# First linear-attention layer computed through G (input times phi of keys), with GpSimd making parts of the keys

## The chip, the cores and the metric

The program runs on one core of a Trainium2 chip. The metric is the device time of one execution in microseconds. Three executions of the kernel before took 1737.16, 1738.05 and 1738.56 us; the median, 1738.05 us, is what the changed kernel is compared with.

## The reference

Four layers in the order A, B, A, B are applied to x of shape 2048 x 640 (32 heads of 20 columns), each as `x = x + layer(layernorm(x))`. Layer A is linear attention with one set of weights for both of its uses:

```python
phi = lambda t: jnp.where(t > 0, t + 1, jnp.exp(t)) + 1e-6
pq, pk = phi(q), phi(k)                      # q, k, v = x @ wqkv, by head
kv = jnp.einsum("bhsd,bhse->bhde", pk, v)
z = jnp.einsum("bhsd->bhd", pk)
num = jnp.einsum("bhqd,bhde->bhqe", pq, kv)
den = jnp.einsum("bhqd,bhd->bhq", pq, z)[..., None] + 1e-6
return (num / den) @ wo
```

Layer B splits the sequence into four segments of 512 rows. Each segment has causal softmax attention by head and, mixed in by a gate, a read of a memory that the earlier segments have written. Nothing of layer B's arithmetic is touched here.

## The kernel before

**Pieces.** x lives in DRAM between layers. A segment is 512 rows, four tiles of 128 rows. Matmuls with f32 accuracy are made of f16 pairs: a value is split into a high and a low f16 part, and three products (high*high, high*low, low*high) are accumulated. `proj_n` (L388) makes one half tile of a projection in natural layout, 128 rows by 320 columns, with 5 x 3 = 15 matmuls of 320 columns; I call this a chain. `proj_t` (L374) makes 128 output columns by 512 rows, transposed, with 15 matmuls of 512 columns. `turn` (L312) transposes a tile with five f32 transposes and writes both f16 parts (ACT the high one, DVE the low one).

**The two ways to compute layer A.** The first layer A uses `a_first` (L695). For each segment it makes values (8 chains, evacuated by one ACT instruction each into v), phi of keys (8 chains, then exponential and relu on ACT, minimum and +1e-6 on GpSimd at L421, sum on DVE at L422) and phi of queries (5 `proj_t`, the same phi at 512 columns, stored to DRAM by GpSimd's queue at L721), and adds phi(keys)^T v, f32 matmuls of 147 or 168 columns (L730), into `acc`. Its second half, `a_second` (L802), reads the queries back, multiplies them with the memory (`a_read` L759 into `read_mem` L439: f32 matmuls at L450, then reciprocal and product on DVE), turns the result and projects it with wo (`o_half` L471).

The second layer A uses `g_first` (L522). Values are never made. For each segment it makes phi of keys (`keys`, 8 chains; ACT exponential and relu, DVE sum at L410, ACT the high f16 part times k_scl at L537, DVE the low part at L538, DVE adds to z at L543), phi of queries in natural layout (`queries`, 8 chains, DVE adds 1e-6 at L549, SP stores to DRAM), and adds x^T phi(keys) into G (`memory`, 10 chains of 12 matmuls at L564; the last operand needs all four tiles of keys). `xs` holds the f16 parts of the normalized x in natural layout, its low part made by GpSimd (L513). After the fourth segment `merge` (L588) scales G by 1/z, multiplies it with wv (L642) and then with wo (L674, L679) into one matrix `wm`. Its second half reads the queries, multiplies them by z and by the reciprocal of their head sums on GpSimd (`p_read` L766: L771, L777, with three small DVE instructions between), turns them and projects with `wm`.

**Order of the work.** PE's instructions run in program order; the order on the other engines is made by a scheduler at build time. The program weaves generators: `weave` (L98) alternates the chains of a main generator with pieces of an auxiliary one. In `opening` (L1149) the main one is the first layer's first half, segment by segment, and the auxiliary ones prepare the eight weight matrices (`w_prep` L228: DMA in, five maximum reductions on DVE at L239, a transpose and a broadcast through PE at L247 and L253, five ACT copies at L263 and five DVE differences at L264, DMA out) and normalize the next segment's x (`moments` L333: two DVE statistics at L338, a power on GpSimd at L343; `normed` L366 on ACT). Before the first chain stand the first tile's transposes and the whole preparation of the first weight. When `opening` has ended, `dense` (L1226) weaves the second half of layer A with layer B's projections (`b_project` L865) segment by segment. A second stream, layer B's attention, starts when B's first segment is projected; `run` (L1307) alternates the streams by accumulated cost. GpSimd masks each exponential tile of the attention (L1059), and PE's weighted sums (L1075) need the masked tile.

The first layer B weaves `b_out` of segment 0 (eight chains, 20 transposes) into the projection of segment 2; the second layer B stores that segment's result instead and does `b_out` at the end. Otherwise both layers B have one form.

## Time and profile before

| what | value |
|---|---|
| median of three runs | 1738.05 us |
| profiled execution, device time | 1736.07 us |
| its span, first to last instruction | 1734.4 us |
| PE busy | 1666.1 us, 96% of the span |
| DVE busy | 1180.9 us, 68% |
| ACT busy | 969.7 us, 56% |
| GpSimd (POOL) busy | 517.7 us, 30% |
| granted TensorE clock | 0.998 |

Times in the rows are microseconds from the start of the span. In the chain of waits and the timeline a row gives its start, its length, the engine, the line and the number of merged records; an f32 matmul that is not a transpose has two records. In groups of instructions the mean of one instruction is in ns, and it includes pipelining: consecutive matmuls follow each other faster than one of them lasts, so that the cost of a chain is read from the chain of waits, where rows follow each other without overlap.

### The profile page before, as it was taken

What the parts mean: (1) busy time and instruction counts of PE and PEld (TensorE: products, weight loads), DVE (VectorE), ACT (ScalarE), POOL (GpSimd) and SP (SyncE); (2) the same over time, 40 slices, a digit from 0 to 9 for tenths busy, and PEclk for the clock granted to TensorE, in tenths of its full rate; (3) what the DMA queues carried; (4) which work ended last, traced back from release to release, by engine and by line L of the source; (5) the groups of instructions that cost most, each with busy time, mean ns of one, the idle gap of its engine ahead of it and who ended that gap; (6) DMA issues with size and microseconds to landing.
All of it is one profiled execution on the core that took longest, in us unless ns stands there. A gap on an engine that the chain in (4) does not pass through costs nothing.

```text
span 1734.4 us, 36014 instructions
## 1 busy us (share of the span) xinstructions
PE 1666.1 (96%) x13032; PEld 1047.5 (60%) x13032; DVE 1180.9 (68%) x3849; ACT 969.7 (56%) x1818; POOL 517.7 (30%) x982
## 2 busy tenths in 40 slices
PE   6999999999999999999999999999999999999998
PEld 4676667664565576556556777666546545645555
DVE  8645534577787677759864456746777877878773
ACT  5545433357557645667675544333665576666673
POOL 1543350012123312334351301221422432233452
PEclk9999999999999999999999999999999999999999
DMA  7522452422322322352211303423232323223432
GB/s 262 184 109 95 150 195 97 139 76 82 113 71 73 113 96 68 120 179 95 78 48 51 103 32 122 175 98 116 75 102 85 112 81 108 93 82 111 131 115 92
DMA packets 118330, 187.58 MB, mean 108 GB/s; under 512 B 13949, under 2 KB 79613, under 8 KB 115849
## 3 DMA queue, kind: packets, MB, share of 16 engines
q1 hardware_dynamic: 105896, 142.68, 25.5%
q0 software_dynamic: 3040, 21.63, 3.4%
q10 hardware_dynamic: 9216, 20.98, 3.1%
q8 instruction: 103, 1.69, 0.4%
q14 instruction: 75, 0.61, 0.1%
HBM read 106.05 MB, written 78.64 MB: 106 GB/s over the span
## 4 chain that ended last, share of the span: by engine, by line
PE 78%; DVE 10%; ACT 6%; issue 2%; POOL 2%; DMA 1%; SPq 1%; ACTq 0%; POOLq 0%; DVEq 0%
PE ps L395 32%; PE ps L381 17%; PE ps L1075 7%; PE ps L1048 4%; ACT pe L1052 3%; PE ps L1007 3%; PE ps L319 3%; PE ps L564 3%; PE ps L450 3%; DVE ps L1013 2%; PE ps L1088 1%; PE ps L891 1%; PE ps L730 1%; DVE st L338 1%; DVE xn L479 1%
## 5 line engine op out<-in xcount | busy, mean ns | idle before, releaser
L1013 DVE CUSTOM_DVE_ANT_0 ps<-ps,maskw 128x512 f32<-128x512 f32 (+3 forms) x1024 | 472.5, 519 | 38.0 <-PE ps L1007 35.7
L1052 ACT ACTIVATE pe<-ps,lsc 128x512 f32<-128x512 f32 x640 | 394.8, 696 | 87.6 <-PE ps L1048 84.9
L1059 POOL TENSOR_SCALAR_AFFINE_SELECT pe<-pe 128x256 f32<-128x256 f32 (+1 forms) x640 | 229.7, 365 | 449.2 <-ACT pe L1052 444.0
L395 PEld LDWEIGHTS <-xT 128*128 128x128 f16 x2880 | 280.3, 98 | 114.6 <-issue 9.3
L395 PEld LDWEIGHTS <-oT 128*128 128x128 f16 x1920 | 185.7, 98 | 80.5 <-issue 7.0
L1075 PE MATMUL ps<-pe,v 128*32 128x512 f32 (+3 forms) x2048 | 162.2, 436 | 11.5 <-POOL pe L1059 5.1
L395 PE MATMUL ps<-w_Bo,oT 128*128 128x320 f16 x960 | 142.3, 302 | 2.8 <-ACT pe L1052 1.1
L1013 DVE DVE_READ_ACCUMULATOR2_ANT mg<- 128x1 f32 x1024 | 143.9, 141 | 0.0
L381 PE MATMUL ps<-xT,w_Bq 128*128 128x512 f16 x600 | 140.2, 380 | 1.9 <-ACT pe L1052 0.8
L395 PE MATMUL ps<-w_Bv,xT 128*128 128x320 f16 x960 | 139.7, 300 | 0.8 <-DVE otok L1095 0.6
L381 PE MATMUL ps<-xT,w_Bk 128*128 128x512 f16 x600 | 138.8, 380 | 1.2 <-ACT pe L1052 1.2
L395 PE MATMUL ps<-w_Ak,xT 128*128 128x320 f16 x960 | 136.1, 300 | 0.0
L1007 PE MATMUL ps<-ks,qs 60*128 60x512 f16 (+3 forms) x1024 | 123.1, 298 | 6.7 <-ACT pe L1052 2.9
L856 DVE SCALAR_TENSOR_TENSOR nat<-ps,nat 128x512 f16<-128x512 f32 x80 | 55.2, 690 | 89.2 <-ACT nat L855 89.1
L1048 PE MATMUL ps<-qs,ks 62*128 62x512 f16 (+3 forms) x1024 | 105.9, 301 | 3.0 <-DMA qs<-mt 1.5
L1075 PEld LDWEIGHTS ps<-pe,v 128*32 128x32 f32 x2048 | 65.3, 109 | 71.9 <-issue 45.8
L421 POOL TENSOR_SCALAR e<-e 128x320 f32<-128x320 f32 (+1 forms) x52 | 82.9, 1594 | 82.4 <-ACT e L417 78.2
L855 ACT ACTIVATE nat<-ps 128x512 f16<-128x512 f32 x80 | 48.2, 603 | 91.8 <-PE ps L381 69.2
L381 PEld LDWEIGHTS <-w_Bk 128*128 128x128 f16 x600 | 57.3, 98 | 65.5 <-issue 5.6
L381 PEld LDWEIGHTS <-w_Bq 128*128 128x128 f16 x600 | 56.7, 98 | 65.9 <-issue 7.8
L1007 PEld LDWEIGHTS <-qs 60*128 60x128 f16 x1024 | 50.0, 94 | 70.9 <-issue 44.7
L343 POOL TENSOR_TENSOR rs<-rs,mhalf 128x1 f32<-128x1 f32 x48 | 27.0, 563 | 218.8 <-DVE rs L342 218.7
(217 smaller groups left out, 2630.7 us busy)
## 6 DMA issues: line engine op xcount, KB each, us to landing
x<-xn ACTq DMA_DIRECT2D x48, 320.0 KB
qs<-qd SPq DMA_DIRECT2D x128, 120.0 KB
ks<-kd SPq DMA_DIRECT2D x128, 120.0 KB
xo<-x SPq DMA_DIRECT2D x48, 320.0 KB
pqi<-pqd SPq DMA_DIRECT2D x32, 320.0 KB
qd<-nat SPq DMA_DIRECT2D x40, 256.0 KB
kd<-nat SPq DMA_DIRECT2D x40, 256.0 KB
x<-in_A_x SPq DMA_DIRECT2D x16, 320.0 KB
```

The costliest lines, as they stand in the source:

```text
L319: nc.tensor.transpose(pt[:, (c - c0) * P:(c - c0 + 1) * P], src[:, c * P:(c + 1) * P], self.ident)
L381: nc.tensor.matmul(p, w[:, c, a, t * P:(t + 1) * P], xT[:, c, b, :], start=k == 0, stop=k == 3 * C - 1)
L395: nc.tensor.matmul(p, xT[:, c, a, i * P:(i + 1) * P], w[:, c, b, n * HN:(n + 1) * HN], start=k == 0, stop=k == 3 * C - 1)
L421: nc.gpsimd.tensor_scalar(e, e, 1.0, eps, op0=OP.min, op1=OP.add)
L450: nc.tensor.matmul(nd[:, lo - k * cut:hi - k * cut], pq[t], mem[:, OFF[t] + lo - a:OFF[t] + hi - a], start=first, stop=True, skip_group_ch ...
L856: nc.vector.scalar_tensor_tensor(nat[:, 1], p, QK_SHIFT, nat[:, 0], op0=OP.mult, op1=OP.subtract)
L1007: nc.tensor.matmul(bs[par][:, a:a + n], qs[r, p, i * P:(i + 1) * P], ks[r, p, :n], start=True, stop=True)
L1013: nc.vector.tensor_tensor_reduce(bs[par][:, a:a + n], bs[par][:, a:a + n], self.maskw[:, SEG - n:], 1.0, NEG, OP.add, OP.max, G["mg"][:, p ...
L1048: nc.tensor.matmul(b[:, a:a + n], ks[r, p, j * P:(j + 1) * P], qs[r, p, j * P:], start=True, stop=True)
L1052: nc.scalar.activation(e, b, AF.Exp, scale=self.lsc)
L1059: nc.gpsimd.affine_select(d, d, pattern=pat, compare_op=OP.is_ge, fill=0.0, base=0, channel_multiplier=-1)
L1075: nc.tensor.matmul(G["pv"][32 * h4:32 * h4 + 32, j * P:], v[j][:, h * E1:h * E1 + 32], G.pop((p, par, j)), start=j == 0, stop=j == 2, skip ...
```

## The change

The first layer A now uses `g_first`, `merge` and `p_read` too; `a_first`, `a_read` and their helpers are gone. In this layer (`early`) three kinds of work of the keys and queries are on GpSimd where the second layer has them on DVE or in ACT's scale: the multiplication by k_scl (which now comes before the high part), the low part and, from the second segment on, the addition to z; GpSimd also adds the 1e-6 to the queries. z then holds scaled keys, and `merge` takes that back with k_inv.

```diff
-                e = self.phi_a(self.proj_n(xT, w["k"], i, n), self.inv["A", "k"])
-                nc.scalar.activation(pk[i][:, 0, c], e, AF.Copy, scale=self.k_scl)
-                nc.vector.scalar_tensor_tensor(pk[i][:, 1, c], e, self.k_scl, pk[i][:, 0, c],
-                                               op0=OP.mult, op1=OP.subtract)
+                e = self.phi_a(self.proj_n(xT, w("k"), i, n), self.inv["A", "k"])
+                hi, lo = pk[i][:, 0, c], pk[i][:, 1, c]
+                if L["early"]:
+                    nc.gpsimd.tensor_tensor(e, e, self.k_scl.to_broadcast([P, HN]), op=OP.mult)
+                    nc.scalar.activation(hi, e, AF.Copy)
+                    nc.gpsimd.tensor_tensor(lo, e, hi, op=OP.subtract)
+                else:
+                    nc.scalar.activation(hi, e, AF.Copy, scale=self.k_scl)
+                    nc.vector.scalar_tensor_tensor(lo, e, self.k_scl, hi, op0=OP.mult, op1=OP.subtract)
+                vec = nc.gpsimd if L["early"] and s > 0 else nc.vector
...
-                nc.vector.tensor_scalar(e, e, 1e-6, None, op0=OP.add)
+                (nc.gpsimd if L["early"] else nc.vector).tensor_scalar(e, e, 1e-6, None, op0=OP.add)
...
+        if L["G"] is None and L["early"]:
+            for i in range(NT):
+                yield from keys(i)
+            yield from memory()
+            for i in range(NT):
+                yield from queries(i)
+            return
...
-        cur = [self.x_t()]
-        v = a("v")
+        cur = [None, self.x_t(), self.xs_t(0)]
+        k = a("k")
...
-                aux = chain(turns(o, later(a("k"))), self.norms(src, 1, nxt, 6), a("q"))
+                aux = chain(turns(o, later(a("q"))), self.norms(src, 1, nxt, 6), a("v"))
...
+                self.w["A", "v"] = self.fetch(("A", "v"))
                 aux = chain(prep(("B", "o")), last(), self.a_head(L, 0, box))
-            yield from weave(self.a_first(s, cur[0], w, L), aux, per=2 if s else 3)
+            yield from weave(self.g_first(s, cur, use, L), aux, per=2 if s else 3)
```

In the opening the first weight prepared is that of the keys, then queries and values (before: values, keys, queries). In the first segment all four tiles of keys come first, then G, then the queries; in the others keys and queries alternate by tile and G follows.

The first place is DVE's order in the first segment, in the stretch where it prepares the second weight (differences at L264; statistics of x at L338, after the change L337; `nb` and `rs` are the small numbers of the layernorm). Before, that weight is the keys' own:

```order
L264 SCALAR_TENSOR_TENSOR w_Ak_239<-stage_240,scl_Ak_338,w_Ak_239 128x640 x2
L342 TENSOR_SCALAR rs_424<-mv_422 128x1
L338 BN_STATS st_431<-x_429 128x6
L264 SCALAR_TENSOR_TENSOR w_Ak_239<-stage_240,scl_Ak_338,w_Ak_239 128x640 x3
L345 TENSOR_SCALAR nb_427<-mv_422,rs_424 128x1
L340 BN_AGGR mv_434<-st_431 128x2
L239 TENSOR_REDUCE wmx_598<-stage_597 128x1
```

After the change the second weight is that of the queries, and the sums of the last keys (e_417 to e_555, L409) and the additions to z (L541) stand between its pieces:

```order
L264 SCALAR_TENSOR_TENSOR w_Aq_257<-stage_258,scl_Aq_387,w_Aq_257 128x640
L541 TENSOR_TENSOR z_93<-z_93,e_417 128x320
L264 SCALAR_TENSOR_TENSOR w_Aq_257<-stage_258,scl_Aq_387,w_Aq_257 128x640 x2
L409 SCALAR_TENSOR_TENSOR e_450<-e_450,r_452 128x320
L264 SCALAR_TENSOR_TENSOR w_Aq_257<-stage_258,scl_Aq_387,w_Aq_257 128x640
L541 TENSOR_TENSOR z_93<-z_93,e_450 128x320
L341 TENSOR_SCALAR rs_482<-mv_480 128x1
L337 BN_STATS st_489<-x_487 128x6
L344 TENSOR_SCALAR nb_485<-mv_480,rs_482 128x1
```

The sums of the segment's last two halves of keys, e_530 and e_555, come seven and nine rows behind these; G's first chain on PE needs e_530, its sixth chain e_555.

The second place is GpSimd's order in the second segment. Before, it has one instruction for each half tile of keys and two (one of them a DMA issue) for each 128 columns of queries:

```order
L421 TENSOR_SCALAR e_1309<-e_1309 128x320
L421 TENSOR_SCALAR e_1335<-e_1335 128x320
L343 TENSOR_TENSOR rs_1556<-rs_1556,mhalf_75 128x1
L343 TENSOR_TENSOR rs_1568<-rs_1568,mhalf_75 128x1
L421 TENSOR_SCALAR e_1375<-e_1375 128x512
L721 DMA pqd0_1_95<-pq_1374 128x512
```

After the change it has three for each half tile of keys (times k_scl, addition to z, low part of pk), one for each half tile of queries, and the low part of xs for each tile of x:

```order
L531 TENSOR_TENSOR e_1323<-e_1323,k_scl_181 128x320
L476 TENSOR_TENSOR xs_1863<-xh_1866,xs_1863 128x640
L541 TENSOR_TENSOR z_93<-z_93,e_1323 128x320
L524 MEMSET pk_2031 128x1
L525 MEMSET pk_2031 128x1
L533 TENSOR_TENSOR pk_1304<-e_1323,pk_1304 128x320
L531 TENSOR_TENSOR e_1348<-e_1348,k_scl_181 128x320
L476 TENSOR_TENSOR xs_1863<-xh_1909,xs_1863 128x640
L541 TENSOR_TENSOR z_93<-z_93,e_1348 128x320
L533 TENSOR_TENSOR pk_1304<-e_1348,pk_1304 128x320
L547 TENSOR_SCALAR e_1378<-e_1378 128x320
```

So a half tile of keys now passes GpSimd, ACT and GpSimd again, and in the first segment DVE's share of it waits in line with the preparation of a weight.

193 lines of the change are left out of this document (58 added, 135 removed).

## The prediction

> **What bounds the kernel now.** I read the page's busy table and its row of PE's busy tenths in 40 slices first, then the opening in stretches of 20 us (columns: stretch, length, busy time and instructions of PE, PE's weight loads, DVE, ACT, GpSimd; granted clock, DMA share, GB/s).
>
> ```profile
> PE 1666.1 (96%) x13032; PEld 1047.5 (60%) x13032; DVE 1180.9 (68%) x3849; ACT 969.7 (56%) x1818; POOL 517.7 (30%) x982
> ...
> PE   6999999999999999999999999999999999999998
> ```
> ```profile
> 0.00:20.00 20.00, 7.16 (x26) 4.25 (x27) 14.18 (x36) 8.11 (x13) 2.80 (x22) 1.00 0.69 244
> 20.00:40.00 20.00, 19.23 (x141) 14.10 (x140) 19.15 (x54) 12.45 (x24) 3.29 (x6) 1.00 0.75 282
> ```
>
> PE is the bound: 96% of the span, and at nine tenths or more in every slice but the first and the last. Its time outside the attention is chains in a fixed order, so work taken from PE shortens the run unless another engine makes PE wait. The exception is the start: PE has 7.2 of the first 20 us, and in the next 20 DVE is as full as PE (19.15 of 20). Both forms of layer A are in this trace, the old in the first layer and the new in the third, so nearly every price has a row.
>
> **PE's work.** The chain of waits (start, length, what) gives the pace of each kind of chain.
>
> ```profile
> 29.64 8.15 PE ps L395 x60
> 187.59 9.71 PE ps L381 x45
> 236.91 5.14 PE ps L730 x40
> 255.14 1.46 PE ps L450 x12
> 271.91 0.55 PE ps L319 x5
> ```
> ```profile
> 976.69 4.92 PE ps L564 x36
> ```
>
> That is 0.1358 us a matmul of 320 columns (2.04 a chain), 0.2158 of 512, 5.14 a segment of the old memory, 1.46 a tile of the old read, 0.11 a transpose, 0.1367 a matmul of G. Removed: values 480 x 0.1358 = 65.2, transposed queries 300 x 0.2158 = 64.7, memory 4 x 5.14 = 20.6, reads 16 x 1.46 = 23.4; together 173.9 us. The projection with wo becomes the same number of matmuls with `wm`, the transposes of the result stay. Added: natural queries 480 x 0.1358 = 65.2, G 480 x 0.1367 = 65.6, and `merge`, which the third layer's timeline shows whole:
>
> ```profile
> 1073.17 1.24 PE L609 MATMUL ps<-z,square 128*128 128x320 f32 x4
> 1074.25 13.28 PE L564 MATMUL ps<-pk,xs 128*128 128x321 f16 x96
> 1087.36 2.20 PE L395 MATMUL ps<-w_Aq,xT 128*128 128x320 f16 x15
> ...
> 1094.90 2.87 PE L395 MATMUL ps<-w_Aq,xT 128*128 128x320 f16 x15
> ...
> 1111.90 1.09 PE L319 MATMUL ps<-ident,pqi 128*128 128x128 f32 x8
> ```
>
> From 1073.17 to 1111.90 are 38.7 us, of which G (96 x 0.1367 = 13.1) and two chains of queries (4.1) are counted already; 21.5 stay, waits on DVE among them. Added 152.3, net **-21.6 us**.
>
> **What layer B gives back.** 14 of the 16 removed reads stand in or between the projections of layer B, where DVE and ACT are busy too and GpSimd now multiplies queries. The third layer has that form already. I compare the starts of B's values of segment 0 and 3, and the start of the projection of layer A's first result, in layers one and two and in layers three and four:
>
> ```profile
> 256.76 1.52 PE L395 MATMUL ps<-w_Ao,oT 128*128 128x320 f16 x10
> ```
> ```profile
> 276.92 2.20 PE L395 MATMUL ps<-w_Bv,xT 128*128 128x320 f16 x15
> ```
> ```profile
> 670.74 1.52 PE L395 MATMUL ps<-w_Bv,xT 128*128 128x320 f16 x10
> ```
> ```profile
> 1113.03 2.53 PE L395 MATMUL ps<-wm,oT 128*128 128x320 f16 x15
> ```
> ```profile
> 1133.05 2.20 PE L395 MATMUL ps<-w_Bv,xT 128*128 128x320 f16 x15
> ```
> ```profile
> 1496.34 0.84 PE L395 MATMUL ps<-w_Bv,xT 128*128 128x320 f16 x5
> ```
>
> From segment 0 to 3 the old form takes 393.8 us, the new one 363.3. Of the 30.5 between them, 18.5 are `b_out` of segment 0, woven in only in the first (8 chains 16.3, 20 transposes 2.2). So 12.0 of the 12 x 1.46 = 17.5 us are really gained; 5.5 go to other waits. From the first projection to B's first values it is 20.2 against 20.0, where two reads (2.9) went: 2.8 back. **+8.3 us.** Bounds: 0, if those waits belong to layer four alone, and 12.
>
> GpSimd's two products per tile, ahead of the masks that PE's L1075 waits for, and the small DVE instructions between them are inside these 8.3, since layers three and four have them.
>
> **The start.** Before, the first eight chains were values: one ACT instruction each, nothing on DVE, and PE could run them while DVE prepared weights and statistics. Now they are keys, each needing two ACT, two DVE and GpSimd instructions, and G starts only when the four tiles have gone through. PE's own pace for eight chains and the transposes stays; by the row at 37.63 it is done at about 38.
>
> ```profile
> 37.63 0.49 PE L319 MATMUL ps<-ident,xh 128*128 128x128 f32 x3
> ...
> 50.22 0.35 PE L253 MATMUL ps<-wm,ones 1*128 1x1 f32 x2 [1.53 <-DVE wm L249]
> 50.50 8.32 PE L395 MATMUL ps<-w_Ak,xT 128*128 128x320 f16 x60
> ```
> ```profile
> 15.58 3.26 DVE L264 SCALAR_TENSOR_TENSOR w_Av<-stage,scl_Av,w_Av 128x640 f16<-128x640 f32 x4
> ```
> ```profile
> L239 DVE TENSOR_REDUCE wmx<-stage 128x1 f32<-128x640 f32 x40 | 31.7, 810 | 6.0 <-DMA stage<-in_B_wk 3.8 <-DMA stage<-in_B_wv 1.8 <-DMA stage<-in_B_wo 0.2
> L338 DVE BATCH_NORM_STATS2 st<-x 128x6 f32<-128x320 f32 x32 | 14.1, 468 | 1.8 <-DMA x<-in_A_x 1.8
> L410 DVE SCALAR_TENSOR_TENSOR e<-e,r 128x320 f32<-128x320 f32 x64 | 32.6, 510 | 45.4 <-ACT r L409 45.3
> L543 DVE TENSOR_TENSOR z<-z,e 128x320 f32<-128x320 f32 x30 | 15.5, 517 | 0.7
> L264 DVE SCALAR_TENSOR_TENSOR w_Aq<-stage,scl_Aq,w_Aq 128x640 f16<-128x640 f32 x5 | 4.4, 919 | 0.9 <-ACT w_Aq L263 0.9
> L324 DVE TENSOR_TENSOR xT<-ps,xT 128x384 f16<-128x384 f32 x64 | 35.3, 551 | 20.6 <-ACT xT L323 20.5
> L324 DVE TENSOR_TENSOR xT<-ps,xT 128x256 f16<-128x256 f32 x64 | 26.6, 416 | 20.2 <-ACT xT L323 19.9
> L342 DVE TENSOR_SCALAR rs<-mv 128x1 f32<-128x1 f32 x48 | 7.1, 148 | 0.9
> ```
>
> The first weight is split at 18.8 in both kernels. From there to the sum of the last keys DVE has in its new order 12 statistics (5.6 us), 6 low parts of xT (2.9), 8 sums (4.1), 6 maxima (4.9), 5 differences of the queries' weight (4.6), 6 additions or copies to z (2.7, taking a copy at half) and some thirty small ones like L342's (4.4): 29.2 us, so 48.0. One product and one difference on GpSimd follow, at 0.87 by its row below: 49.7. Only the last three of a chain's twelve matmuls need that tile, so PE's solid run starts as if 9 x 0.1367 = 1.2 earlier, at 48.5; I take 49 for some waiting, and before it was 50.5. But at 50.5 PE had four more chains (8.15) and 17 more transposes (1.9) behind it. So the start costs 49 - 50.5 + 10.0 = **+8.5 us**. Bounds: DVE's instructions overlap by a tenth and it never waits, 45.6, +5.1; it waits for ACT, whose copies of the high part wait for GpSimd in line ahead of the next exponential, by 5 us in all, 54, +13.5.
>
> **The rest of the opening** I cost at zero. GpSimd's work per later segment:
>
> ```profile
> L477 POOL TENSOR_TENSOR xn<-xn,xo 128x320 f32<-128x320 f32 x56 | 48.7, 870 | 143.2 <-ACT xn L476 138.8 <-issue 2.9 <-POOL pe L1059 0.8
> L421 POOL TENSOR_SCALAR e<-e 128x320 f32<-128x320 f32 x32 | 43.0, 1344 | 56.2 <-ACT e L417 53.1 <-DVE wm L249 1.5 <-DVE w_Aq L264 1.4
> L513 POOL TENSOR_TENSOR xs<-xh,xs 128x640 f16<-128x640 f32 x16 | 22.4, 1415 | 11.8 <-ACT xs L512 11.8
> ```
>
> 24 two-operand instructions at 0.87 or less, 8 additions of 1e-6 between half of 1.34 (one operation in place of two) and 1.34, 4 low parts at 1.41 and about 2 for powers: 34 to 39 us. PE's segment is 16 chains, G's 16.4 and 20 transposes, 51.2 us. So GpSimd fits on average; in the keys and queries alone it has 8 to 10 us a tile against PE's 8.7, so it falls a little behind and recovers under G. What waits: ACT's copy of the high part, with the next exponentials and the copies of xT behind it, for whom PE has eight banks of room; and PE's first G chain. SP now stores 32 half tiles of queries, each waiting for GpSimd's addition, and behind them are queued the loads of x and of B's weights, for which DVE's maxima and then PE wait. A wait of that kind is there already:
>
> ```profile
> 154.87 0.76 PE L319 MATMUL ps<-ident,xh 128*128 128x128 f32 x5 [1.87 <-DVE xT L324]
> ```
>
> GpSimd is rid of the 20 DMA issues of L721. Bounds: -1.9 (that stall goes) to +6 (one more such in each of the three segments).
>
> **Sum.** -21.6 + 8.3 + 8.5 + 0 = -4.8. The profiled execution took 1736.07 (span 1734.4), 1.98 under the median of the runs shown; 1736.07 - 4.8 + 1.98 = 1733.2, said as 1733.
>
> **Rivals.**
> *GpSimd becomes the bound of segments 1 to 3 of the opening; slower.* Where DVE and GpSimd both read two operands, GpSimd can take longer:
>
> ```profile
> 134.56 2.47 DVE L264 SCALAR_TENSOR_TENSOR split<-stage,scl_Bv,split 128x640 f16<-128x640 f32 x3
> ...
> 136.23 2.58 POOL L421 TENSOR_SCALAR e<-e 128x512 f32<-128x512 f32 x1 [4.56 <-ACT e L417]
> ```
> ```profile
> L421 POOL TENSOR_SCALAR e<-e 128x512 f32<-128x512 f32 x20 | 39.9, 1996 | 26.2 <-ACT e L417 25.2
> ```
>
> 2.58 beside DVE's differences where the mean is 2.00. If GpSimd stood still through all of DVE's such work (16 sums at 0.51, 5 to 10 differences at 0.92, 13 to 17 us a segment), 39 would become 52 to 56, over PE's 51.2 by up to 5 a segment. It decides from 51 us on; three segments give up to +15: 1738 to 1748, middle 1743. Against it: 0.6 lost in one instruction beside 2.5 of differences, not all of it, and not every DVE instruction meets one. Chance 0.15. The Trainium skill (SBUF — State Buffer, "Who interferes with whom") has the rule behind this: a DVE instruction with two SBUF inputs and a GpSimd instruction that reads SBUF share a read interface, whoever starts first holds it for the whole instruction and the other fully blocks. By that rule the upper end, 1748, would be nearer; the trace shows less than a full block.
>
> *The start costs its upper bound*, +13.5 to 14: 1738 to 1739, no change. For it: DVE's new order mixes sums that wait for ACT with weights that wait for ACT. 0.20.
>
> *Layer B gives back nothing*: 1725. For it: the fourth layer's waits need not recur in the second, whose projections have other neighbours. 0.20.
>
> *The forecast*, 1729 to 1737: 0.45.
>
> **How the numbers follow.** 0.2% (3.5 us) is about what a measurement can tell from no change. Faster by more: 0.36 of the forecast, 0.20 of the third rival, 0.02 of the second, 0.58. Within: 0.07 + 0.13 + 0.02 = 0.22. Slower: 0.13 of the first, 0.05, 0.02, 0.20. The range goes from 1723, the third rival with a little of the other lower bounds, to the first rival's middle, 1743.
>
> **What will show it.** Right: PE idle between about 38 and 49 with G's first chain behind the low part of keys; segments 1 to 3 of 51 to 54 us each with PE full; B's values of segment 0 starting at 281 to 285, and 380 to 384 us from them to those of segment 3. Wrong: GpSimd busy 9 tenths from 85 to 240 with PE waiting on it; PE waiting for the exponentials' banks; the first G chain after 54; a stall at the weight loads.

## The result and the profile after

The changed kernel takes **1756.82 us** (median of four, 1756.03 to 1759.48) against 1738.30 for the kernel before beside it (the three executions above and a fourth, 1739.73): ratio 1.0109, interval 1.0091 to 1.0126. It is slower by 18.5 us. The profiled execution's span is 1754.4, 20.0 more than before. First the busy table, PE's busy tenths and its granted clock:

```profile
PE 1659.4 (95%) x13032; PEld 1033.9 (59%) x13032; DVE 1231.1 (70%) x3908; ACT 991.2 (56%) x1883; POOL 604.6 (34%) x1117
...
PE   6889989999999999999999999999999999999998
...
PEclk9989989999999999999999999999999999999999
```

Eights where nines stood in the second, third and sixth slice, and eights in the clock in the third and sixth: all in the opening, before 264 us. The opening by segment, before and after (stretch, length, busy time and instructions of PE, PE's loads, DVE, ACT, GpSimd; clock, DMA share, GB/s); the stretches end where the next segment's first keys start (before: its first values), with the projection of the first result, and with B's values:

```profile
0.00:80.16 80.16, 64.79 (x406) 43.45 (x407) 59.99 (x154) 43.69 (x78) 27.41 (x45) 1.00 0.63 224
80.16:137.20 57.04, 57.04 (x382) 38.81 (x381) 30.66 (x70) 28.80 (x54) 24.42 (x22) 1.00 0.29 108
137.20:197.31 60.11, 57.76 (x384) 39.01 (x383) 31.41 (x58) 28.56 (x56) 25.70 (x19) 1.00 0.40 145
197.31:256.76 59.45, 59.45 (x402) 41.70 (x401) 21.38 (x48) 23.28 (x44) 27.72 (x25) 1.00 0.46 158
256.76:276.92 20.16, 20.16 (x157) 15.78 (x155) 14.52 (x42) 5.94 (x12) 4.15 (x5) 1.00 0.62 204
```
```profile
0.00:88.87 88.87, 65.55 (x409) 44.81 (x410) 68.61 (x170) 53.69 (x96) 44.79 (x82) 0.94 0.54 194
88.87:153.39 64.52, 57.46 (x388) 40.01 (x386) 34.83 (x74) 30.53 (x63) 41.88 (x54) 0.92 0.33 114
153.39:208.14 54.75, 52.79 (x388) 38.05 (x386) 35.02 (x69) 27.59 (x59) 29.49 (x36) 1.00 0.41 145
208.14:289.73 81.59, 72.13 (x545) 47.65 (x543) 58.14 (x120) 35.02 (x77) 42.22 (x49) 0.94 0.44 163
289.73:309.75 20.02, 19.52 (x142) 14.00 (x143) 12.33 (x34) 4.96 (x12) 4.29 (x5) 1.00 0.64 226
```

B's values start 32.8 us later (309.75 against 276.92). PE is idle for 42.3 us until there (lengths less busy times), before for 17.7: 24.6 more. Its busy time is 8.2 longer (267.5 against 259.2, the sums of the columns), though by the prediction's prices it has 4.1 less work there (152.3 added, 173.9 less the 17.5 of twelve later reads removed): some 12 us, an estimate by these prices, are matmuls at a lower clock (the clock column allows 15.4). From there to the end the changed kernel is 12.8 faster, 1444.6 against 1457.5. So the whole loss is made in the opening.

What the lower clock looks like, in PE's timeline of the second segment:

```profile
120.82 2.20 PE L394 MATMUL ps<-w_Ak,xT 128*128 128x320 f16 x15
126.69 0.55 PE L253 MATMUL ps<-wm,ones 1*128 1x1 f32 x2 [3.67 <-DVE wm L249]
127.17 4.18 PE L394 MATMUL ps<-w_Ak,xT 128*128 128x320 f16 x15
131.15 5.08 PE L394 MATMUL ps<-w_Aq,xT 128*128 128x320 f16 x30
```

After a wait of 3.67 us the next chain takes 4.18 in place of 2.20, and the two after it 5.08 in place of 4.24. Last, whom ACT and GpSimd wait for from 88 to 260 us (waits: total, times, longest):

```profile
ACT pk L532 <- POOL e L531: 48.0, 21, 7.2
```
```profile
POOL e L531 <- DVE e L409: 25.8, 14, 8.5
POOL e L547 <- DVE e L409: 14.1, 17, 4.4
```

ACT stands at the copy of the high part until GpSimd's product is there, and behind the copy stand the next exponentials; DVE's sums wait for those and GpSimd for DVE's sums. I call this the ring. GpSimd has 41.88 us of work in the 64.52 of the second segment, but not evenly: while the segment's last keys and queries go through, it is nearly full, 18.67 of 20 us, with PE at 16.10:

```profile
120.00:140.00 20.00, 16.10 (x96) 10.55 (x94) 10.77 (x19) 13.65 (x27) 18.67 (x20) 0.83 0.08 30
```

### The profile page after: what moved, and what is told of

The parts are those of the page before. It is cut to its first block, busy times and chain, and to the rows that moved or that the text cites. A ratio compares the mean times of both kernels' runs of the same rounds, so it can differ in the third digit from the quotient of the medians.

```text
span 1754.4 us, 36272 instructions
## 1 busy us (share of the span) xinstructions
PE 1659.4 (95%) x13032; PEld 1033.9 (59%) x13032; DVE 1231.1 (70%) x3908; ACT 991.2 (56%) x1883; POOL 604.6 (34%) x1117
## 3 DMA queue, kind: packets, MB, share of 16 engines
q1 hardware_dynamic: 102312, 147.93, 25.6%
## 4 chain that ended last, share of the span: by engine, by line
PE 64%; DVE 12%; ACT 7%; POOL 6%; issue 3%; DMA 2%; SPq 0%; ACTq 0%; POOLq 0%; DVEq 0%
PE ps L394 25%; PE ps L380 13%; PE ps L996 7%; PE ps L969 3%; PE ps L928 3%; ACT pe L973 3%; PE ps L318 3%; PE ps L562 3%; DVE ps L934 2%; PE ps L445 2%; PE ps L813 2%; PE ps L1009 1%; POOL e L547 1%; POOL e L531 1%; DVE xn L471 1%
## 5 line engine op out<-in xcount | busy, mean ns | idle before, releaser
L934 DVE CUSTOM_DVE_ANT_0 ps<-ps,maskw 128x384 f32<-128x384 f32 (+3 forms) x1024 | 472.7, 518 | 39.5 <-PE ps L928 36.8
L394 PEld LDWEIGHTS <-xT 128*128 128x128 f16 x2880 | 282.7, 99 | 121.3 <-issue 10.7
L394 PE MATMUL ps<-w_Ak,xT 128*128 128x320 f16 x960 | 144.0, 307 | 5.4 <-DVE w_Ak L264 2.2
L562 PE MATMUL ps<-pk,xs 128*128 128x321 f16 (+1 forms) x960 | 143.3, 307 | 6.1 <-POOL pk L533 3.2
L394 PE MATMUL ps<-wm,oT 128*128 128x320 f16 x960 | 141.7, 299 | 1.9
L394 PE MATMUL ps<-w_Aq,xT 128*128 128x320 f16 x960 | 139.5, 302 | 1.6 <-DVE xT L323 1.2
L409 DVE SCALAR_TENSOR_TENSOR e<-e,r 128x320 f32<-128x320 f32 x128 | 71.1, 559 | 84.8 <-ACT r L408 83.0
L562 PEld LDWEIGHTS <-xs 128*128 128x128 f16 x960 | 95.2, 100 | 47.4 <-issue 8.9
L996 PEld LDWEIGHTS ps<-pe,v 128*32 128x32 f32 x2048 | 65.5, 109 | 74.5 <-issue 39.3
L469 POOL TENSOR_TENSOR xn<-xn,xo 128x320 f32<-128x320 f32 x56 | 49.0, 876 | 145.3 <-ACT xn L468 141.1
```

The source lines that it names most:

```text
L394: nc.tensor.matmul(p, xT[:, c, a, i * P:(i + 1) * P], w[:, c, b, n * HN:(n + 1) * HN], start=k == 0, stop=k == 3 * C - 1)
L409: nc.vector.scalar_tensor_tensor(e, e, 1.0, r, op0=OP.min, op1=OP.add)
L562: nc.tensor.matmul(p, xs[:, i, a, c * P:(c + 1) * P], pk[i][:, b, cols], start=k == 0, stop=k == 3 * NT - 1)
L934: nc.vector.tensor_tensor_reduce(bs[par][:, a:a + n], bs[par][:, a:a + n], self.maskw[:, SEG - n:], 1.0, NEG, OP.add, OP.max, G["mg"][:, p ...
L996: nc.tensor.matmul(G["pv"][32 * h4:32 * h4 + 32, j * P:], v[j][:, h * E1:h * E1 + 32], G.pop((p, par, j)), start=j == 0, stop=j == 2, skip ...
```

## The experiments

All times are in us. The stages are read from each run's PE timeline: start of the second segment's first keys (before: values), lengths of segments 2 and 3, of segment 4 with `merge`, and the start of B's values. Each ratio is to executions of the kernel before beside the run (their medians are 1736.9 to 1738.7).

| run | median | ratio to before (interval) | seg. 2 starts | seg. 2 | seg. 3 | seg. 4, merge | B's values |
|---|---|---|---|---|---|---|---|
| before | 1738.05 | | 80.2 | 57.0 | 60.1 | 59.4 | 276.9 |
| after | 1756.8 | 1.0109 (1.0091-1.0126) | 88.9 | 64.5 | 54.8 | 81.6 | 309.8 |
| e1_hi_direct | 1757.4 | 1.0117 (1.0102-1.0133) | 86.6 | 69.1 | 53.9 | 80.6 | 310.1 |
| e2_all_dve | 1738.2 | 1.0000 (0.9990-1.0010) | 88.1 | 53.5 | 53.6 | 71.9 | 287.1 |
| e3_q_dve | 1748.5 | 1.0059 (1.0042-1.0076) | 90.6 | 59.1 | 54.1 | 77.4 | 301.1 |
| e4_s0_mixed | 1756.7 | 1.0112 (1.0097-1.0127) | 93.3 | 60.0 | 54.9 | 80.8 | 309.0 |
| e5_queries_first | 1734.2 | 0.9974 (0.9965-0.9983) | 88.9 | 53.5 | 53.7 | 73.3 | 289.4 |
| e6_idle_pool | 1760.9 | 1.0124 (1.0109-1.0138) | 88.3 | 65.0 | 58.5 | 79.9 | 311.7 |
| e7_z_q_dve | 1745.0 | 1.0037 (1.0024-1.0050) | 89.8 | 57.4 | 54.3 | 73.6 | 295.0 |
| e8_warm | 1759.8 | 1.0124 (1.0111-1.0137) | 91.0 | 65.0 | 56.7 | 80.2 | 312.9 |
| e9_relu_psum | 1750.8 | 1.0075 (1.0061-1.0089) | 89.2 | 62.9 | 55.0 | 75.7 | 302.8 |
| e10_writes_only | 1754.3 | 1.0095 (1.0079-1.0110) | 98.2 | 62.0 | 53.8 | 71.9 | 305.9 |
| e11_v_later | 1752.4 | 1.0081 (1.0067-1.0095) | 85.9 | 52.2 | 54.8 | 84.0 | 304.5 |
| e12_direct_psum | 1749.9 | 1.0067 (1.0052-1.0082) | 87.3 | 66.6 | 54.4 | 74.5 | 302.9 |
| e13_const_later | 1748.9 | 1.0069 (1.0055-1.0082) | 87.7 | 67.2 | 53.4 | 75.2 | 303.5 |
| e14_direct_psum_q | 1735.8 | 0.9988 (0.9977-0.9999) | 86.5 | 54.2 | 56.4 | 72.0 | 289.2 |
| e15_pinned_writes | 1741.0 | 1.0020 (1.0011-1.0029) | 87.8 | 58.8 | 53.6 | 73.4 | 293.7 |
| e16_v_later_2 | 1754.6 | 1.0093 (1.0077-1.0108) | 86.8 | 52.2 | 60.4 | 82.6 | 302.1 |
| e17_best | 1741.8 | 1.0020 (1.0010-1.0030) | 92.0 | 52.5 | 57.2 | 71.8 | 293.5 |
| e18_stores_pool | 1748.3 | 1.0057 (1.0042-1.0073) | 86.7 | 64.4 | 52.2 | 76.5 | 299.8 |

### Which part of the change costs

**e1_hi_direct**: ACT no longer waits for GpSimd; every engine keeps its work.

```diff
+                    nc.scalar.activation(hi, e, AF.Copy, scale=self.k_scl)
                     nc.gpsimd.tensor_tensor(e, e, self.k_scl.to_broadcast([P, HN]), op=OP.mult)
-                    nc.scalar.activation(hi, e, AF.Copy)
```

> Same instructions on every engine; ACT writes the high part straight from phi of the keys with the scale in its own instruction, and GpSimd's product comes behind it, so that GpSimd waits for ACT and no longer ACT for GpSimd. Theory 1 (ring: ACT, in line, stands at the copy of the high part until GpSimd's product is done, 48.0 us in 21 waits between 88 and 260 us, and the exponentials behind it keep PE's banks): PE's idle time in segments 1 to 3 (16.9 us from 88.9 to 267.2) and the slow clock after it (8.4) go almost all: 1731 to 1738 us. Theory 2 (GpSimd has simply too much work): its work is unchanged, 1753 to 1760 us. Theory 3 (the stores of queries hold SP's loads back): nothing changes there, 1753 to 1760 us.

Nothing gained: theory 1 in this form falls. ACT's wait for GpSimd is gone, but ACT now stands at the same copy for DVE's sum, and the sums have got longer, 801 ns against 624 in the changed kernel (see e6). So the edit takes away one wait, puts another in its place and lengthens the sums. The sums from 88 to 255 us and ACT's wait from 88 to 260:

```profile
L409 DVE SCALAR_TENSOR_TENSOR e<-e,r 128x320 f32<-128x320 f32 x49 | 39.0, 801 | 22.9 <-ACT r L408 20.1 <-POOL z L541 2.9
```
```profile
ACT pk L531 <- DVE e L409: 38.9, 20, 6.3
```

And PE now waits at G for the low part itself; from 120 to 140 us GpSimd is busy for 19.36 of 20. Of PE's waits in the first 300 us (in the changed kernel the upper one is 3.2, the lower 2.4):

```profile
PE ps L562 <- POOL pk L533: 10.5, 3, 7.2
...
PE ps L614 <- POOL square L610: 5.2, 1, 5.2
```

**e2_all_dve**: `early` off, so that the arithmetic is placed as in the second layer A; the order of the first segment stays.

```diff
-        return dict(z=z, G=None, pqd=pqd, zb=None, wm=None, early=n == 0)
+        return dict(z=z, G=None, pqd=pqd, zb=None, wm=None, early=False, first=n == 0)
```

> The first layer A with the arithmetic placed as in the second: scale in ACT's copy, low part, addition to z and 1e-6 on DVE, GpSimd with none of it; the order of the chains stays that of the changed kernel. Theory 1 (ring): ACT no longer waits for GpSimd, DVE has some 13 us more per segment and 48 of 54: 1730 to 1740, like the direct high part to within 4. Theory 2 (GpSimd's load): as good, but the direct high part alone stays at 1753 to 1760. If DVE is what counts then, it becomes the bound and the time is over 1745.

The whole loss goes: 1738.2, no difference from before. Segments 2 and 3 take 53.5 and 53.6 with PE idle for 1.1 and 1.2. The start is as late as in the changed kernel. GpSimd's arithmetic is the cause of the 22.6 us between the two at B's values. Segments 2 to 4 have 21.8 of them: PE stands there for 18.5 us in the changed kernel and 5.7 here, and its work takes 182.4 against 173.4, at a clock of 0.92, 1.00 and 0.94 against 1.00. But without it the change is worth nothing either: B's values start 10.2 later than before, 7.9 of it at the start, and the rest is 8.4 shorter. (This rest varies from 1443.6 to 1449.0 us between the runs, whose code is the same there; differences of B's values are the finer measure.)

**e3_q_dve** and **e7_z_q_dve** take it back piecewise: the 1e-6, then (last two lines) the addition to z too.

```diff
-                (nc.gpsimd if L["early"] else nc.vector).tensor_scalar(e, e, 1e-6, None, op0=OP.add)
+                nc.vector.tensor_scalar(e, e, 1e-6, None, op0=OP.add)
...
-                vec = nc.gpsimd if L["early"] and s > 0 else nc.vector
+                vec = nc.vector
```

> Only the 1e-6 of the queries goes back to DVE: GpSimd has 8 to 10 us less per segment, and the stores of queries no longer wait for GpSimd. Theory 1 (ring): the copy of the high part still waits for GpSimd's product, only with less work ahead of it: 1748 to 1756. Theory 2 (load): a quarter of GpSimd's work goes, and a third to a half of the loss, 1742 to 1748. Theory 3 (the stores hold SP's loads back): most of the waits at loads go, 1740 to 1748.

> Of the changed kernel's GpSimd work only the product and the low part stay (13 us a segment in place of 34 to 39); 1e-6 and the addition to z go to DVE. ACT still waits for the product. If GpSimd's amount of work is what counts, the loss against the run with all of it on DVE goes nearly whole: 1738 to 1743. If it is the step from engine to engine (DVE, GpSimd, ACT, GpSimd, PE), half of it stays: 1744 to 1750.

At B's values 8.6 and 14.7 of the 22.6 us are back. The less GpSimd has, the smaller the loss, which is theory 2's side; but the product and the low part alone still cost 8, and e7's 1745.0 lies in the range for the step from engine to engine. DVE's sums take 629 ns in e3, as in the changed kernel, and 532 in e7, so that e7's gain may come from shorter sums as well as from less work.

**e4_s0_mixed** gives the first segment the others' order.

```diff
-        if L["G"] is None and L["early"]:
+        if False:
```

> Only the first segment's order: keys and queries by tile in turn and G at the end, as in the other segments, in place of all keys, G, queries. If the order makes the late start (23.4 us of idle PE and 4.3 of slow clock until 72.6 us), PE has the queries' chains to run while the keys are made, and 5 to 9 us go: 1747 to 1752. If the ring makes it, the queries' exponentials stand behind the copies as well: 1754 to 1762.

No change in time. The second segment starts 4.4 later and is 4.5 shorter; PE waits for the queries' weight instead.

### What GpSimd's work does to others

**e6_idle_pool** is e2 with additions on a tile that nobody reads, as many as the changed kernel gives GpSimd (`hi` is only read):

```diff
+                if L["first"] and s > 0:
+                    for _ in range(3):
+                        nc.gpsimd.tensor_tensor(self.sc1, self.sc1, hi, op=OP.add)
```

> All arithmetic on DVE and ACT again, and beside it GpSimd makes as many additions of 128x320 as the changed kernel gives it in segments 2 to 4, on a tile of its own that nobody reads. If GpSimd costs by being waited for (its results are late), nobody waits here: 1736 to 1741, and segments of 53 to 55 us. If it costs by holding up DVE's reads, DVE's instructions get longer and segments 2 to 4 go to 57 or more: 1746 to 1756.

1760.9, above the range of either expectation: with nobody waiting for its results GpSimd costs as much as in the changed kernel, 24.6 us at B's values against e2. DVE's groups from 88 to 255 us tell why (count, busy, mean ns): first e2, then this run, then the changed kernel.

```profile
L409 DVE SCALAR_TENSOR_TENSOR e<-e,r 128x320 f32<-128x320 f32 x51 | 25.9, 508 | 6.7 <-ACT r L408 6.3
...
L323 DVE TENSOR_TENSOR xT<-ps,xT 128x384 f16<-128x384 f32 x8 | 4.4, 547 | 0.0
L264 DVE SCALAR_TENSOR_TENSOR split<-stage,scl_Ao,split 128x640 f16<-128x640 f32 x5 | 4.3, 878 | 0.0
```
```profile
L411 DVE SCALAR_TENSOR_TENSOR e<-e,r 128x320 f32<-128x320 f32 x50 | 38.9, 778 | 0.8 <-ACT r L410 0.8
...
L266 DVE SCALAR_TENSOR_TENSOR split<-stage,scl_Ao,split 128x640 f16<-128x640 f32 x5 | 6.4, 1295 | 0.0
...
L325 DVE TENSOR_TENSOR xT<-ps,xT 128x384 f16<-128x384 f32 x8 | 4.4, 545 | 0.0
```
```profile
L409 DVE SCALAR_TENSOR_TENSOR e<-e,r 128x320 f32<-128x320 f32 x50 | 31.0, 624 | 39.2 <-ACT r L408 37.6 <-POOL z L541 0.8 <-issue 0.3
...
L264 DVE SCALAR_TENSOR_TENSOR split<-stage,scl_Ao,split 128x640 f16<-128x640 f32 x5 | 6.6, 1354 | 0.1
```

Instructions that read two tensors in SBUF (the sums, the weights' differences) get longer beside GpSimd, 508 to 778 ns and 878 to 1295; the difference for xT, whose one operand is in PSUM, does not (547 and 545). I call this lengthening the collision.

**e10_writes_only** and **e15_pinned_writes** ask whether it is GpSimd's reading. Both replace the additions by memsets of 128x320. In e10 nothing ties them to their place; in e15 a copy of one column of `hi` ahead of each bunch does:

```diff
+        self.nc.gpsimd.tensor_copy(self.sc1[:, :1], hi[:, :1])
+        for _ in range(k):
+            self.nc.gpsimd.memset(self.sc1, 1.0)
```

> As the run with idle GpSimd additions (1760.9), with all real arithmetic on DVE and ACT, but GpSimd only writes: 72 memsets of 128x320 a segment into a tile of its own, in place of the additions that read two tiles. Theory C (reads collide): DVE's sums stay at 500 to 520 ns, and the time is that of the run with all arithmetic on DVE, 1736 to 1742. Theory Q (a busy GpSimd delays the low parts of x and the powers that queue behind the idle work): as slow as with the additions, 1755 to 1762.

> As the run with idle GpSimd additions (1760.9), with the same places and about the same busy time, but GpSimd's idle work only writes: after a read of one column of the keys' high part, 8 or 10 memsets of 128x320 a half tile (0.378 us each). Theory C (reads collide): DVE's sums stay at 500 to 520 ns, low parts at 545 to 585, and the time is that of all arithmetic on DVE or a little more, 1737 to 1743. Theory Q (a busy GpSimd is late with the low parts of x and the powers): 1754 to 1762.

e10 doesn't answer: its memsets ran early, and the start is 10 us later (98.2). e15 does. GpSimd's idle work between 88 and 255 us is as long as in e6, whose groups come first, 89.1 and 88.9 us:

```profile
L541 POOL TENSOR_TENSOR sc<-sc,pk 128x320 f32<-128x320 f32 x72 | 68.0, 944 | 37.4 <-ACT pk L537 33.0
L554 POOL TENSOR_TENSOR sc<-sc,pk 128x320 f32<-128x320 f32 x24 | 21.1, 880 | 1.8
```
```profile
L704 POOL MEMSET sc<- 128x320 f32 x216 | 80.3, 372 | 12.0
L702 POOL CAST sc<-pk 128x1 f32<-128x1 f16 x24 | 8.6, 357 | 19.1 <-ACT pk L537 17.9
```

DVE's two-operand instructions in e15 keep their lengths:

```profile
L411 DVE SCALAR_TENSOR_TENSOR e<-e,r 128x320 f32<-128x320 f32 x50 | 26.2, 524 | 6.9 <-ACT r L410 6.7
...
L266 DVE SCALAR_TENSOR_TENSOR split<-stage,scl_Ao,split 128x640 f16<-128x640 f32 x5 | 4.3, 876 | 0.0
```

Its addition of 1e-6 to the queries, one tensor and a constant, does not; in e2, e6 and e15:

```profile
L547 DVE TENSOR_SCALAR e<-e 128x320 f32<-128x320 f32 x27 | 9.5, 352 | 0.4
```
```profile
L552 DVE TENSOR_SCALAR e<-e 128x320 f32<-128x320 f32 x26 | 15.9, 612 | 0.4
```
```profile
L551 DVE TENSOR_SCALAR e<-e 128x320 f32<-128x320 f32 x26 | 12.3, 474 | 0.4
```

18 of e6's 24.6 us at B's values are gone; the 6.6 left are what a GpSimd busy with writes costs, these longer additions among them. The rule is in the Trainium skill (SBUF — State Buffer, "Who interferes with whom"): a DVE instruction with two SBUF inputs contends with a GpSimd instruction that reads SBUF, not with one that only writes it. For the two-operand instructions these runs agree in both halves.

**e9_relu_psum** takes the collision from the changed kernel's sums, in segments 2 to 4:

```diff
-        r = sb.tile([P, 512], F32, tag="er", name="r", bufs=3)[:, :HN]
+        r = p if self.inplace else sb.tile([P, 512], F32, tag="er", name="r", bufs=3)[:, :HN]
         nc.scalar.activation(r, p, AF.Relu, scale=inv)
```

> The changed kernel, but in segments 2 to 4 ACT writes relu back into the PSUM bank it read, and DVE's sum of phi takes its second operand from PSUM in place of SBUF; GpSimd's work is untouched. Theory C (GpSimd's reads and DVE's two-operand reads of SBUF hold each other up, as the sums of 624 ns in the changed kernel, 508 with all arithmetic on DVE and 778 beside idle GpSimd additions say): the sums go back to about 500 ns, GpSimd's additions to 0.87, and 5 to 10 us go: 1746 to 1752. Theory L (GpSimd's results are simply late, through the ring DVE, GpSimd, ACT): the sums get shorter and the time stays, 1754 to 1759.

The sums fall to 481 ns (second operand `ps`), with GpSimd's work unchanged, and 6.9 us come back at B's values, 6.0 in the median. That is theory C's side, but GpSimd's additions did not get shorter (941 ns for z, 949 in the changed kernel).

```profile
L410 DVE SCALAR_TENSOR_TENSOR e<-e,ps 128x320 f32<-128x320 f32 x46 | 22.0, 481 | 39.8 <-ACT ps L409 37.5 <-issue 0.7 <-POOL z L543 0.7
```

### What is left without the collision of the sums

**e12_direct_psum** joins e1 and e9; **e14_direct_psum_q** adds e3.

> The changed kernel with both: the high part written straight from phi with ACT's scale, so that ACT does not wait for GpSimd, and relu back into PSUM, so that DVE's sum reads SBUF once. GpSimd's amount of work is the changed kernel's. If collision and ring together are the cause, each enough to hide the other's removal, nearly the whole loss of segments 2 to 4 goes: 1738 to 1745. If GpSimd's amount of work is a cause of its own, half stays: 1746 to 1752.

> The run with the direct high part and relu in PSUM (1749.9), and the 1e-6 of the queries on DVE: GpSimd keeps product, addition to z and low part (about 20 us a segment), and SP's stores wait for DVE. Theory G (GpSimd's amount) and theory S (SP's stores) both expect most of the remaining 12 us against all arithmetic on DVE to go: 1739 to 1744. If the three instructions of the keys alone make GpSimd late, 1746 to 1750.

e12 gains nothing over e9: 1749.9 misses 1738 to 1745 and lies in the range for GpSimd's amount of work. e14 is at 1735.8, below both of its ranges, the whole loss gone, though GpSimd keeps the product, z and the low part (62 us from 88 to 255 by its groups, against 91 with the 1e-6 in the changed kernel). The end of the second segment shows the amount: GpSimd is full there in e12, and PE stands for 5.7 us for its low part; in e14 it is half idle and PE stands for 1.0. First e12, then e14:

```profile
120.00:140.00 20.00, 14.18 (x89) 9.31 (x88) 10.63 (x21) 13.03 (x26) 19.27 (x21) 0.85 0.07 25
```
```profile
120.00:140.00 20.00, 19.04 (x140) 13.42 (x138) 14.41 (x28) 7.29 (x13) 9.44 (x11) 1.00 0.52 192
```

By themselves e12 gives 6.9 and e3 8.6 us at B's values, together 20.6: the parts hide each other. Whether the direct high part has a share is not shown: alone (e1) and on top of e9 (e12) it gained nothing, and e14 without it was not run. The weights' differences still collide in e14, and the loss is gone all the same:

```profile
L265 DVE SCALAR_TENSOR_TENSOR split<-stage,scl_Ao,split 128x640 f16<-128x640 f32 x5 | 7.2, 1470 | 0.0
```

The 1e-6 is work for GpSimd, and the queries' stores wait for it on SP, with loads behind them. **e13_const_later** moves the load that DVE stood for in e12; **e18_stores_pool** lets GpSimd issue the stores. The edits to e12:

```diff
-                aux = chain(self.norms(src, 2, nxt, 6), a("o"), late(), prep(("B", "v"), False))
+                aux = chain(self.norms(src, 2, nxt, 6), a("o"), prep(("B", "v"), False))
...
-                aux = chain(self.norms(src, 3, nxt, 6), prep(("B", "q"), False), prep(("B", "k"), False))
+                aux = chain(self.norms(src, 3, nxt, 6), prep(("B", "q"), False), prep(("B", "k"), False), late())
```
```diff
-                nc.sync.dma_start(L["pqd"][s][i][:, n * HN:(n + 1) * HN], e)
+                (nc.gpsimd if L["early"] else nc.sync).dma_start(L["pqd"][s][i][:, n * HN:(n + 1) * HN], e)
```

> The run with the direct high part and relu in PSUM (1749.9), of whose remaining 16 us nearly all lie in the second segment, with the constants for layer B (the mask's and the blocks' load and their two casts on DVE) moved to the end of the third segment's weights. There DVE stood 4.0 us at the mask's cast, for a load that SP had queued behind two stores of queries, which wait for GpSimd. Theory S (stores ahead of loads on SP start the second segment late): 4 to 7 us go, 1743 to 1746. Theory G (GpSimd's amount of work is late at the segment's end whatever starts it): 1748 to 1752.

> The run with the direct high part and relu in PSUM (1749.9), with the stores of the queries issued by GpSimd in place of SP: SP's loads of x and weights no longer stand behind stores that wait for GpSimd, and GpSimd has eight issues a segment more, some 5 us (0.626 each in the kernel before). Theory S (SP's stores ahead of the loads hold the second segment): 1740 to 1745. Theory G (GpSimd's amount of work holds it): 1750 to 1756.

e13 changes nothing (1748.9). Of the next two rows the first is e12's wait from 55 to 140 us, the others e13's from 75 to 150: the wait passed to the next loads.

```profile
DVE maskw L185 <- DMA cst<-in_const: 4.0, 1, 4.0
```
```profile
DVE st L338 <- DMA x<-in_A_x: 7.0, 2, 4.4
...
DVE wmx L240 <- DMA stage<-in_B_wv: 5.9, 3, 4.4
```

e18 gets 3.0 us at B's values although GpSimd has 15.6 us more; the waits for loads go, and PE waits for GpSimd's low part instead, above all at the end of the second segment:

```profile
PE ps L565 <- POOL pk L535: 11.1, 2, 8.3
```

The time fits neither theory's range: both effects are there, and how the 1e-6's share divides between them stays open.

### The slow clock

**e8_warm** puts 56 matmuls of zeros where PE stood in the second and fourth segment, e.g. in the bank of the broadcast:

```diff
+        warm = 24 if key == ("A", "o") else 0
+        for k in range(warm):
+            nc.tensor.matmul(pb[:, :HN], self.ident16, self.zero, start=k == 0, stop=False, skip_group_check=True)
```

> The changed kernel with 56 more matmuls of zeros on PE, which add nothing to the sums: 24 (3.3 us) ahead of the broadcast of wo's maximum in the second segment, where PE stood 3.7 us, 16 (2.2) inside the fourth segment's first G chain and 16 ahead of the sum of z, where it stood 2.1, 1.5 and 2.4. PE has 7.6 us more work and less idle time. If the slow clock after such waits costs its own time (8.3 us in segments 2 to 4), the granted clock stays at 1.00 there and 3 to 6 us go: 1751 to 1754. If PE is held by GpSimd's results anyway, a faster PE only waits longer: 1755 to 1759.

The clock is 0.95 in the second segment in place of 0.92, 0.97 in the third (1.00) and 0.98 in the fourth (0.94). PE's idle time in these segments falls from 18.5 to 13.5 us, and nothing is gained: 1759.8, just above the second expectation's range, which speaks for PE being held by others' results. The clock did not stay at 1.00, though, so that the first is not ruled out for a kernel in which it does.

### A version that beats both

**e5_queries_first**: e2's arithmetic, and the first segment in the order queries, keys, G.

```diff
+            for i in range(NT):
+                yield from queries(i)
+            w("k")
+            self.key_scale()
             for i in range(NT):
                 yield from keys(i)
             yield from memory()
-            for i in range(NT):
-                yield from queries(i)
             return
...
-        k = a("k")
+        k = a("q")
```

> The arithmetic as in the second layer (no keys on GpSimd, as in the run before with all of it on DVE, 1738.2), and the first segment in the order queries, keys, G, with the queries' weight prepared first. Theory 1 (the start is late because G needs all keys before PE has a second weight): PE has 16 chains before the first G chain, the second weight is ready at 52 to 54 as in the kernel before (50.5) plus eight sums, and the second segment's first keys start at 80 to 83 in place of 88.1: 1730 to 1734. Theory 2 (the start is bound by DVE, 73.9 of 88 us busy, whatever the order): 1736 to 1741.

1734.2, 0.9974 of before (0.9965 to 0.9983): faster than both kernels. But neither theory's reason is seen: the second segment starts at 88.9, no earlier than e2's. The profiled execution took 1738.0, the longest of its twelve, so the profile doesn't show where the 4 us come from; that stays open. **e11_v_later** and **e16_v_later_2** move the preparation of the values' weight out of the first segment, **e17_best** joins e5 and e14. The lists of segments 1 to 3 in e16, against e5 (in e11 layer B's `k` stands ahead of its `o` in the fourth, and `late()` behind A's `o`):

```diff
-                aux = chain(turns(o, later(a("k"))), self.norms(src, 1, nxt, 6), a("v"))
+                aux = chain(turns(o, later(a("k"))), self.norms(src, 1, nxt, 6))
...
-                aux = chain(self.norms(src, 2, nxt, 6), a("o"), late(), prep(("B", "v"), False))
+                aux = chain(self.norms(src, 2, nxt, 6), a("v"), a("o"))
...
-                aux = chain(self.norms(src, 3, nxt, 6), prep(("B", "q"), False), prep(("B", "k"), False))
+                aux = chain(self.norms(src, 3, nxt, 6), late(), prep(("B", "v"), False), prep(("B", "q"), False), prep(("B", "k"), False))
```

> As the run with queries first (1734.2), with the preparation of the values' weight, which only merge needs, moved from the first segment to the second, and those of layer B each a segment later where they were two. DVE has 8 to 9 us less in the first 88 us. If DVE bounds the start (83 of the first 100 us busy), PE's idle and slow time there (29.7 us) falls by 4 to 8: 1726 to 1731. If the order of waits on ACT and DVE bounds it, or the moved weights hold up the second and fourth segment: 1733 to 1739.

> As the run with queries first and the values' weight moved to the second segment, whose first three segments ended at 193.0 in place of 196.1 us, but with three weights of layer B in the third segment, so that the fourth has only B's output weight as in the run with queries first (its fourth segment took 73.3, the other's 84.0). If DVE has room for the third weight in the third segment (about 44 of 53.6 us busy, 9 more): 1729 to 1733. If not, the third segment takes 57 or more: 1735 to 1740.

> The run of 1735.8 (high part direct, relu in PSUM, 1e-6 on DVE, GpSimd with product, sum of z and low part) with the first segment in the order queries, keys, G. Measured apart, the first stands 0.1% below the kernel before, the order 0.2% below the kernel with its own arithmetic. If the two add: 1730 to 1733. If the order gains nothing of its own (its second segment began no earlier, 88.9 against 88.1 us): 1734 to 1738.

The weight moved: the second segment starts 3.0 and 2.1 earlier than in e5 and then takes 52.2, PE never idle. So DVE's load has a small part in the start. But the displaced weights cost 10.7 (e11) and 9.3 (e16) in the fourth segment, in e16 6.7 in the third too, in e11 7.6 more before B's values (27.6 against 20.0 from the first projection), and PE waits for their maxima. Both times lie above both of their ranges. Of e16:

```profile
PE ps L247 <- DVE wm L244: 12.7, 2, 7.5
```

e17 starts its second segment at 92.0 and is at 1741.8, above both of its ranges: the two gains don't add, and why is open.

## Why the prediction was wrong, point by point

- **PE bound, and the work removed**: held where GpSimd has none of the work. In e2, which has the same chains, segments 2 and 3 (1 and 2 in the prediction's count) take 53.5 and 53.6, inside the 51 to 54 forecast; in the changed kernel they take 64.5 and 54.8. From B's values to the end 12.8 us went, where 12.0 were expected (17.5 for twelve reads, less the 5.5 given back); in the other runs, whose code is the same there, it was 8.4 to 13.9.
- **Layer B**: held. From B's values of segment 0 to segment 3 it is 383.0 (380 to 384 forecast), and from the first projection to the first values 20.0, as in layer three:

```profile
309.75 2.20 PE L394 MATMUL ps<-w_Bv,xT 128*128 128x320 f16 x15
```
```profile
692.73 2.20 PE L394 MATMUL ps<-w_Bv,xT 128*128 128x320 f16 x15
```

- **The start, +8.5**: the first chain of G begins at 48.31 (49 forecast), but it is not a solid run. PE stands again for the last keys, whose low part is there at 53.5 (49.7 forecast), and the clock is lower. Twelve matmuls of G take 3.32 at 54.69 and 1.81 at 58.72:

```profile
48.31 2.62 PE L562 MATMUL ps<-pk,xs 128*128 128x321 f16 x9
51.80 0.30 PE L562 MATMUL ps<-pk,xs 128*128 128x321 f16 x1 [0.87 <-ACT pk L532]
53.50 0.43 PE L562 MATMUL ps<-pk,xs 128*128 128x321 f16 x2 [1.39 <-POOL pk L533]
...
54.69 3.32 PE L562 MATMUL ps<-pk,xs 128*128 128x321 f16 x12
...
58.72 1.81 PE L562 MATMUL ps<-pk,xs 128*128 128x321 f16 x12
```
```profile
40.00:60.00 20.00, 14.03 (x81) 9.42 (x80) 15.95 (x36) 13.93 (x27) 11.73 (x17) 0.83 0.49 170
```

  The first segment has 4.9 us less PE work (values 16.3, transposed queries 16.2 and memory 5.1 go, queries 16.3 and G 16.4 come), so the forecast put the second at 80.2 + 8.5 - 4.9 = 83.8; it began at 88.87. The start cost 13.6, the second rival's price. From G's first chain to the second segment the forecast has 34.8 us (83.8 less 49), and it took 40.6 (88.87 less 48.31). PE stood for 2.3 us of that, and the clock, which the working left at 1.00, took some 3.0 more (0.74 from 48.31 to 60.00: 0.26 x 11.7). The keys were late in part because DVE waited: it had 26.1 us of work from 18.8 to the last sum at 50.7, less than the 29.2 counted, and stood for 5.8, of which 4.4 for GpSimd's products and powers. The rival has DVE wait too, but for ACT.
- **"The rest of the opening I cost at zero"**: this is the step that failed. The forecast put B's values at 276.9 - 4.1 + 8.5 + 2.8 = 284.1. Of the 25.6 us to 309.75 the start has 5.1 and segments 2 to 4 have 20.5, against bounds of -1.9 to +6. The step compared GpSimd's sum of work, 34 to 39 us, with PE's 51.2 and found that it fits. The sum was nearly right (41.9, 29.5 and 42.2 us of busy time), but fitting over the segment was not the condition. GpSimd does this work while the keys and queries are made, and at the end of the second segment's it is full (18.67 of 20 us from 120 to 140). What the step called falling a little behind is the stretch in which PE stands and its clock falls to 0.83. In the fourth segment PE stands for the last keys and GpSimd (2.1, 1.5 and 2.4 us at G and the sum of z), and the clock is 0.74 from 240 to 260. And the step left DVE's sums at 0.51, which GpSimd's reads lengthened to 624 ns. By the runs the sums are worth 6.9 us (e9) and the 1e-6 8.6 (e3), and both, with the direct high part, 20.6 of the 22.6 that GpSimd's arithmetic costs (e14). ACT's wait for GpSimd, 48.0 us, was worth nothing by itself, neither with the collision of the sums (e1) nor without it (e12 over e9).
- **The first rival** named the collision and the right side, with a chance of 0.15 and 1738 to 1748. It priced only GpSimd's time, up to 5 us a segment over PE's, and the runs have the lengthening on DVE's side: sums of 624 for 508 ns, while GpSimd's two-operand instructions of 128x320 took 765 to 949 where the prediction had 870. It was to decide from 51 us of GpSimd's work on; there were 41.9 and 29.5 in segments 2 and 3, GpSimd was full in a part of the segment only, and e6 shows that it need not be waited for at all. The rule that the prediction quotes from the Trainium skill put the time nearer 1748 and was the better guide than the one pair of rows (2.58 beside 2.00) set against it, in which GpSimd's instruction read one tensor and not two.
- **What was costed at nothing**: SP's stores ahead of the loads were named and priced as one stall; moving one such load only moved the wait (e13).

## What to carry to other kernels

Before work is moved to GpSimd, list DVE's instructions with two operands in SBUF that run beside it: here they got longer by a quarter to two thirds, and a second operand in PSUM avoided it. An engine that is two thirds busy over a stage can be full in a part of it and hold the others there; look at short stretches, not at the share alone. A long wait need not be what costs: ACT's 48.0 us for GpSimd went in e1, where ACT then stood for DVE instead (38.9), and nothing was gained. Where several causes hide one another, undoing one alone shows little, so undo them together before giving one up.

## What the runs showed of the hardware that was not expected

- DVE's two-operand sums: 508 ns with GpSimd nearly idle, 524 beside memsets, 624 to 801 beside GpSimd instructions that read; 481 with one operand in PSUM. DVE's addition of a constant, one operand: 352 ns with GpSimd nearly idle, 474 beside memsets, 612 beside additions.
- PE's clock halves after short idle times: after 3.67 us without work a chain took 4.18 in place of 2.20. The Trainium skill (TensorE: Matmul & The Clock Gate, "What's actually happening") says that one idle window of some 3.4 us halves the clock and as long a busy one restores it. The rows at 126.69 to 131.15 agree with the first; the slow stretch is longer than one such window, some 6.8 us by the clock of 0.83 from 120 to 140 (0.17 x 20 = 3.4 lost, at half speed). Nor was an unbroken wait of that length needed: after waits of 0.87 and 1.39 us, at 51.80 and 53.50, the clock, 1.00 from 52.31 to 54.31, was 0.51 from 54.31 to 56.31. Raising the clock from 0.92 to 0.95 and from 0.94 to 0.98 with more matmuls gave nothing where PE was held by others' results (e8).
